# W_down's last row in two column pieces, and the output in column groups of 360 and 216

## The chip, the cores and the metric

The kernel runs on one core of a Trainium2 chip. The metric is the device time of one execution in microseconds (us). The kernel before takes 377.71 us, the median of three runs (377.70, 377.71 and 377.72).

## The reference

One decoding step of a transformer block for a batch of 4, in bfloat16: attention over the last 4096 positions of a cache (32 query heads on 16 key/value heads of 128), a residual, and then a gated feed-forward part whose last product is the one that the change touches. Cut to what matters:

```python
def _B_ref(x, W_gate, W_up, W_down):          # x: 4 x 1 x 576
    gate = jnp.einsum("bsd,df->bsf", x, W_gate)   # 576 x 4608
    up = jnp.einsum("bsd,df->bsf", x, W_up)       # 576 x 4608
    gate = gate * (gate > 0)
    h = gate * up
    return jnp.einsum("bsf,fd->bsd", h, W_down)   # 4608 x 576

x = A_x
h = x + _A_ref(_layernorm(x), A_k_cache, A_v_cache, A_wq, A_wo)
h2 = h + _B_ref(_layernorm(h), B_W_gate, B_W_up, B_W_down)
return h2
```

Of the caches and weights some 160 MB are read, each once.

## The kernel before, in words

The program writes the list of operations of every engine by hand. Each operation names what it depends on, and the function `emit` turns this into semaphore waits; an engine then works through its list in that order. All large transfers are issued from one queue, that of SyncE (SP), in the order in which `place` (line 216) is called. `place` also makes a transfer wait for the last reader of the part of the on-chip arena that it overwrites.

The work goes in this order. The query projection comes first. Then 16 tiles of K and 16 of V (4 MB each) pass through four slots of the arena: VectorE transposes a K tile (line 424), TensorE forms the scores, the softmax follows, and TensorE multiplies with V. Then come the output projection with Wo, the second layer norm (lines 627 to 647), the gate and up products (lines 651 to 677), and two transposes on VectorE (line 679), which lay the hidden vector out as 36 blocks of 128 (`hhT`).

The down projection is the last loop (lines 683 to 707). W_down's 4608 rows are laid out as 128 partitions of 36 rows each, so that a "row" r in the text is one row of 576 columns on each of 128 partitions, 147 KB. For each r from 0 to 35 there are two matmuls, n = 0 and n = 1, each with the same 128x32 stationary block of `hhT` and with its own share of the 576 columns as the moving operand. Group 0 (columns 0 to 271) writes to PSUM bank 0, partitions 0 to 31, and group 1 (columns 272 to 575) to bank 1, partitions 32 to 63; these positions put them in different 32-column strips of TensorE's array. Both accumulate over all 36 rows. Before row 0 come six matmuls that add the residual. In the last row the two weight loads are issued ahead of the matmuls (line 699), and the matmuls are made by `mm_same` (line 33), so that they are reported at line 34.

W_down arrives in five transfers, at rows 0, 15, 25, 32 and 35 (`WD_ROWS`, line 280); the matmul of group 0 at those rows waits for its piece. At the end VectorE copies group 0 to the output tile as bfloat16 (`OUT0`, line 708), ScalarE copies group 1 (`OUT1`, line 709), and SP sends the tile out when both are done (line 710).

Of the kernel before, what the change touches and what calls it, by code (L numbers as in the profile page):

```python
# [12 lines left out]
D = 576  # L13
# [19 lines left out]
def mm_same(e, out, lhsT, rhs, start, stop, tile, pos):  # L33
    return e.add_instruction(mybir.InstMatmult(  # L34
        name=e.bass.get_next_instruction_name(), engine=mybir.EngineType.PE, ins=[e.lower_ap(rhs), e.lower_ap(lhsT)],
        outs=[e.lower_ap(out)], start_tensor_calc=start, stop_tensor_calc=stop, tile_size=tile, tile_position=pos,
        ldweights=False, bass_skip_group_check=True))
# [83 lines left out]
def bass_sequential_preLN__sliding_block_cached__glu_gated_reglu__decode_kernel(  # L121
# [12 lines left out]
    with ExitStack() as es:  # L134
        cnt = [0]

        def sb(name, shape, dt):
            return es.enter_context(nc.sbuf_tensor("sb_" + name, shape, dt))
# [3 lines left out]
        dve = lambda name, fn, deps=(): P.op("vector", name, fn, deps)  # L142
        act = lambda name, fn, deps=(): P.op("scalar", name, fn, deps)
# [5 lines left out]
        arena = sb("arena", [128, AW], BF16)  # L149
# [41 lines left out]
        out_sb = sb("out_sb", [32, D], BF16)  # L191
# [14 lines left out]
        bank = [psb[:, i, :] for i in range(8)]  # L206
# [9 lines left out]
        def place(name, off, size, reader, make, key=None):  # L216
            deps = []
            for blk in range(off // 64, (off + size) // 64):
                r = owner.get(blk)
                if r is not None and r not in deps:  # L220
                    deps.append(r)
                owner[blk] = reader
            semk = key or "d_" + "_".join(str(v) for v in name)
            P.dma("sync", ("L",) + name, make, semk, deps)
            land[name] = off
# [37 lines left out]
        for g in range(NTILE - 4, NTILE):  # L263
# [6 lines left out]
            out=bass.AP(tensor=arena, offset=off, ap=[[2 * AW, 64], [1, F]]), in_=B_W_gate[512:576, :]))  # L270
        P.dma("sync", ("L", "gu", 1, 4), lambda e, off=off: e.dma_start(
            out=bass.AP(tensor=arena, offset=AW + off, ap=[[2 * AW, 64], [1, F]]), in_=B_W_up[512:576, :]), "d_gu_1_4")
        gu_off[(0, 4)] = gu_off[(1, 4)] = off
        off += F
        for g, m, n, src in ((0, 0, 4 * F, main_rows(B_W_gate)), (1, 0, 3 * F, main_rows(B_W_up)[:, 0:3 * F]),
# [1 line left out]
            gu_off[(g, m)] = off  # L277
            place(("gu", g, m), off, n, ("GU", g, m), lambda e, off=off, n=n, src=src: e.dma_start(out=arena[:, off:off + n], in_=src))
            off += n
        WD_ROWS = (0, 15, 25, 32, 35, 36)  # L280
        wd_off = off
        for r0, r1 in zip(WD_ROWS, WD_ROWS[1:]):
            place(("wd", r0), wd_off + r0 * D, (r1 - r0) * D, ("DOWN", 1),
                  lambda e, r0=r0, r1=r1: e.dma_start(
                      out=arena[:, wd_off + r0 * D:wd_off + r1 * D],
                      in_=B_W_down.rearrange("(p r) n -> p (r n)", p=128)[:, r0 * D:r1 * D]))


        pool("c_eps", lambda e: e.memset(eps_c[:, :], EPS))
# [15 lines left out]
                                                in_=c_qm[:, :, :].rearrange("p q (h j) -> p q h j", j=4),  # L305
# [4 lines left out]
                                                in_=to_v[:, :, :].rearrange("p n (k a) -> p n k a", a=4),  # L310
# [14 lines left out]
        for sg in range(2):  # L325
            pool(f"c_toq{sg + 1}", lambda e, sg=sg: e.affine_select(
                out=toq[:, :, :, :], in_=toq[:, :, :, :],
# [213 lines left out]
        def finish_o():  # L541
            for q in range(4):
                for qd in range(4):
# [17 lines left out]
                                              in_=bass.AP(tensor=e8, offset=0, ap=[[8, 128], [0, 4], [1, 8]])), ["c_e8", "c_selc0"])  # L561
# [47 lines left out]
        for a in range(8):  # L609
            for n in range(2):  # L610
                for j in range(4):
# [4 lines left out]
                    else:  # L616
# [6 lines left out]
                                             in_=bass.AP(tensor=psb, offset=512 + 224, ap=[[4096, 128], [1, 64], [0, 2]])), ["part1"])  # L623
# [27 lines left out]
        for g in range(2):  # L651
            for c in (4, 0, 1, 2, 3):
                part_ = c if c == 4 or (c == 3 and g) else 0
                for m in range(3):
                    for j in range(4):
                        first = m == 0 and j == 0 and (c in (0, 4) or part_ == 3)
                        deps = [("L", "gu", g, part_)] if first else []
                        if c == 4 and g == 0 and first:
                            deps += [("L", "gu", 1, 4), "n2", "n3", "part0", "partd", ("EXP", B - 1), ("MAX", B - 1)]
                        lo = gu_off[(g, part_)] + (c - part_) * F + 1152 * j + 384 * m  # L660
# [17 lines left out]
        for i in range(2):  # L678
            dve(("HHT", i), lambda e, i=i: e.transpose(
                out=hhT[:, 576 * i:576 * i + 576].rearrange("p (r q) -> p r q", q=32),  # L680
                in_=bass.AP(tensor=pp, offset=3712 + 18 * i, ap=[[PPW, 128], [1, 18], [36, 32]])), [("HH", m) for m in range(3)])

        ncol = ((0, 272), (272, 576))

        def down(n, lhsT, w, start, stop, held=False):
            lo, hi = ncol[n]
            out_ = bank[n][32 * n:32 * n + 32, 0:hi - lo]
            if held:
                return lambda e: mm_same(e, out_, lhsT, w[:, lo:hi], start, stop, (128, 32), (0, 32 * n))
            return lambda e: e.matmul(out_, lhsT=lhsT, rhs=w[:, lo:hi], start=start, stop=stop, skip_group_check=True)  # L690
# [5 lines left out]
        for r in range(36):  # L696
            if r == 35:
                for n in range(2):
                    pe(None, lambda e, n=n: e.ldweights(hhT[:, 32 * 35:32 * 36], tile_position=(0, 32 * n)))
            for n in range(2):  # L700
                deps = []
                if n == 0:
                    if r in WD_ROWS:
                        deps.append(("L", "wd", r))
                    if r % 18 == 0:
                        deps.append(("HHT", r // 18))
                pe(("DOWN", n), down(n, hhT[:, 32 * r:32 * r + 32], arena[:, wd_off + r * D:wd_off + r * D + D], False, r == 35, r == 35), deps)
        dve("OUT0", lambda e: e.tensor_copy(out=out_sb[:, 0:272], in_=bank[0][0:32, 0:272]), [("DOWN", 0)])
        act("OUT1", lambda e: e.copy(out=out_sb[:, 272:576], in_=bank[1][32:64, 0:304]), [("DOWN", 1)])  # L709
        P.dma("sync", "O", lambda e: e.dma_start(out=out.rearrange("b s d -> (b s) d"), in_=out_sb[0:B, :]), "d_out", ["OUT1", "OUT0"])  # L710
        P.op("sync", None, None, ["O"])
        P.emit(nc, es)
# [28 lines left out]
```

## Time and profile before

| | before |
|---|---|
| median of the runs | 377.71 us |
| span of the profiled execution | 377.0 us |
| mean granted TensorE clock | 0.796 of full speed |
| mean DMA rate over the span | 424 GB/s |
| TensorE matmul busy | 213.8 us (57%) |
| VectorE busy | 228.8 us (61%) |
| ScalarE busy | 53.7 us (14%) |
| last W_down piece issued, and its time to landing | 342.69 us, 32.0 us |
| output transfer issued | 375.64 us |

The profiled execution's own time is known only as its span, from its first to its last instruction; the runs are timed without a profile, and 0.7 us lie between the two. Times in the profile count from the start of the span. A busy share is an average over the whole execution and says little of its last stretch; there the chain of waits and the order of time are to be read. "PEclk" is the clock that TensorE was granted, as a share of full speed.

### The profile page before, as it was taken

What the parts mean: (1) busy time and instruction counts of PE and PEld (TensorE: products, weight loads), DVE (VectorE), ACT (ScalarE), POOL (GpSimd) and SP (SyncE); (2) the same over time, 40 slices, a digit from 0 to 9 for tenths busy, and PEclk for the clock granted to TensorE, in tenths of its full rate; (3) what the DMA queues carried; (4) which work ended last, traced back from release to release, by engine and by line L of the source; (5) the groups of instructions that cost most, each with busy time, mean ns of one, the idle gap of its engine ahead of it and who ended that gap; (6) DMA issues with size and microseconds to landing.
All of it is one profiled execution on the core that took longest, in us unless ns stands there. A gap on an engine that the chain in (4) does not pass through costs nothing.

```text
span 377.0 us, 2556 instructions
## 1 busy us (share of the span) xinstructions
PE 213.8 (57%) x1462; PEld 39.9 (11%) x694; DVE 228.8 (61%) x164; ACT 53.7 (14%) x84; POOL 10.5 (3%) x29
## 2 busy tenths in 40 slices
PE   0404443239919091749282844664655787886658
PEld 0000000001001010001010100110000101002316
DVE  4088878779292969584847778665749433333240
ACT  3093000211000114010101140101010411112010
POOL 8200000000000000000000000000000000000000
PEclk9966666659969788696877786989695968998686
DMA  8999999999999999999999999999999999999996
GB/s 334 445 445 428 405 445 442 396 442 445 398 435 445 442 433 403 442 445 435 407 436 445 435 414 431 441 438 431 417 442 438 426 417 442 418 433 437 427 414 256
DMA packets 6378, 159.74 MB, mean 424 GB/s; under 512 B 728, under 2 KB 864, under 8 KB 1248
## 3 DMA queue, kind: packets, MB, share of 16 engines
q1 hardware_dynamic: 6360, 159.59, 98.7%
q8 instruction: 8, 0.13, 0.1%
q14 instruction: 2, 0.02, 0.0%
q10 hardware_dynamic: 8, 0.00, 0.0%
HBM read 159.58 MB, written 0.00 MB: 423 GB/s over the span
## 4 chain that ended last, share of the span: by engine, by line
DMA 60%; PE 20%; DVE 18%; SPq 1%; issue 0%; ACT 0%
DMA sb_arena<-in_A_k_cache_dram 53%; DVE sb_arena L424 16%; PE psb L34 11%; DMA sb_arena<-in_B_W_down_dram 7%; PE psb L448 4%; PE psb L509 3%; PE psb L690 2%; DVE sb_o_tmp L522 1%; DVE sb_pp L487 1%; SPq L242 0%; PE psb L475 0%; SPq L255 0%; ACT sb_out_sb L709 0%; SPq L251 0%; DVE sb_f L534 0%
## 5 line engine op out<-in xcount | busy, mean ns | idle before, releaser
L424 DVE STREAM_TRANSPOSE sb_arena<-sb_arena 128x8192 f32<-128x8192 f32 (+1 forms) x19 | 139.9, 7366 | 67.3 <-DMA sb_arena<-in_A_k_cache_dram 67.3
L448 PE MATMUL psb<-sb_arena 128*32 128x512 bf16 x256 | 42.8, 633 | 119.6 <-DVE sb_arena L424 119.5
L34 PE MATMUL psb<-sb_arena,sb_pp 128*128 128x512 bf16 (+1 forms) x386 | 108.7, 392 | 0.0
L509 PE MATMUL psb<-sb_arena,sb_pp 128*128 128x512 bf16 x128 | 50.8, 397 | 8.9 <-DVE sb_o_tmp L522 8.9
L519 ACT COPY sb_o_tmp<-psb 32x512 f32<-32x512 f32 x32 | 18.5, 577 | 182.0 <-PE psb L34 181.7
L34 PE MATMUL psb<-sb_arena 128*32 128x512 bf16 x256 | 43.6, 642 | 0.0
L522 DVE TENSOR_TENSOR sb_o_tmp<-psb,sb_fm 32x512 f32<-32x512 f32 x32 | 21.7, 678 | 18.6 <-PE psb L34 18.1
L448 PEld LDWEIGHTS psb<-sb_arena 128*32 128x32 bf16 x256 | 9.5, 119 | 161.9 <-DVE sb_arena L424 132.7
L509 PEld LDWEIGHTS psb<-sb_arena,sb_pp 128*128 128x128 bf16 x128 | 12.8, 100 | 116.6 <-issue 116.6
L526 DVE TENSOR_REDUCE sb_o_sel<-sb_o_tmp 128x128 f32<-128x512 f32 x16 | 17.7, 1106 | 0.5
L467 ACT ACTIVATE sb_pp<-psb,sb_hx 128x1024 bf16<-128x1024 f32 x4 | 4.5, 1113 | 79.4 <-DVE sb_hx L464 79.4
L487 DVE TENSOR_TENSOR sb_pp<-psb,sb_m 128x1024 bf16<-128x1024 f32 x8 | 9.3, 1206 | 4.9 <-PE psb L475 4.9
L482 ACT ACTIVATE sb_pp<-psb,sb_m 128x512 bf16<-128x512 f32 x16 | 9.7, 690 | 14.9 <-PE psb L475 14.9
L525 DVE TENSOR_TENSOR sb_o_tmp<-sb_o_tmp,sb_fm 64x512 f32<-64x512 f32 x16 | 11.0, 689 | 0.5
L415 ACT COPY sb_arena<-sb_q_keep 32x256 bf16<-32x256 bf16 x8 | 9.7, 1451 | 0.1
L690 PE MATMUL psb<-sb_arena,sb_pp 128*32 128x272 bf16 (+1 forms) x70 | 7.6, 396 | 3.7 <-DMA sb_arena<-in_B_W_down_dram 3.7
L401 DVE CAST sb_pp<-psb 128x512 bf16<-128x512 f32 x1 | 2.4, 2427 | 10.5 <-PE psb L381 10.5
L470 DVE STREAM_TRANSPOSE sb_pp<-sb_pp 128x1024 bf16<-128x1024 bf16 x4 | 5.0, 1245 | 5.1 <-ACT sb_pp L467 5.1
L475 PE MATMUL psb<-sb_pp,sb_to_v 128*32 128x256 bf16 x64 | 4.3, 400 | 6.3 <-DVE sb_pp L470 6.3
L690 PEld LDWEIGHTS psb<-sb_arena,sb_pp 128*32 128x32 bf16 x70 | 6.0, 131 | 5.1 <-DMA sb_arena<-in_B_W_down_dram 3.9
L34 PE MATMUL psb<-sb_arena,sb_hnT 128*32 128x384 bf16 x80 | 6.5, 407 | 0.0
L381 PE MATMUL psb<-sb_arena,sb_xnT 128*32 128x512 bf16 x16 | 2.6, 628 | 6.3 <-DMA sb_arena<-in_A_wq_dram 6.3
(120 smaller groups left out, 81.5 us busy)
## 6 DMA issues: line engine op xcount, KB each, us to landing
sb_arena<-in_A_k_cache_dram SPq DMA_DIRECT2D x16, 4096.0 KB, 26.3
sb_arena<-in_A_v_cache_dram SPq DMA_DIRECT2D x16, 4096.0 KB, 28.5
sb_arena<-in_A_wo_dram SPq DMA_DIRECT2D x1, 4608.0 KB, 24.8
sb_arena<-in_B_W_gate_dram SPq DMA_DIRECT2D x1, 4608.0 KB, 27.7
sb_arena<-in_A_wq_dram SPq DMA_DIRECT2D x1, 4096.0 KB, 12.7
sb_arena<-in_B_W_up_dram SPq DMA_DIRECT2D x1, 3456.0 KB, 27.3
sb_arena<-in_B_W_down_dram SPq DMA_DIRECT2D x1, 2160.0 KB, 26.5
sb_arena<-in_B_W_down_dram SPq DMA_DIRECT2D x1, 1440.0 KB, 29.6
```

The costliest lines, as they stand in the source:

```text
L34: return e.add_instruction(mybir.InstMatmult(name=e.bass.get_next_instruction_name(), engine=mybir.EngineType.PE, ins=[e.lower_ap(rhs), e. ...
L415: act("QW", lambda e, i=i, q=q: e.copy(out=bass.AP(tensor=arena, offset=32 * i * AW + 2 * i + q, ap=[[AW, 32], [512, 16], [136, 4], [32, 4]]),
L424: dve(("TRA", g), lambda e: e.transpose(out=dst, in_=src), [("L", "K", g)] if lo == 0 else [])
L448: fn = lambda e, out_=out_, lhsT=lhsT, rhs=rhs, start=start, stop=stop: e.matmul(out_, lhsT=lhsT, rhs=rhs, start=start, stop=stop, skip_gr ...
L482: act(("EV", b, 0), lambda e, a=a: e.activation(out=bass.AP(tensor=pp, offset=2 * a, ap=[[PPW, 128], [8, 2], [32, 128], [1, 2]]), in_=bank ...
L487: dve(("EV", b, 1), lambda e, n=n: e.tensor_tensor(out=bass.AP(tensor=pp, offset=16 + 8 * n, ap=[[PPW, 128], [32, 128], [2, 4], [1, 2]]), ...
L509: fn = lambda e, lhsT=lhsT, rhs=rhs, k=k, j=j: e.matmul(bank[2 + j], lhsT=lhsT, rhs=rhs, start=(k == 0), stop=(k == 7), skip_group_check=True)
L519: act(("OSC", g), lambda e, j=j: e.copy(out=o_tmp[32 * j:32 * j + 32, 0:512], in_=bank[2 + j][32 * j:32 * j + 32, :]), [("PV", g), ("OSEL" ...
L522: dve(("OSD", g), lambda e, j=j: e.tensor_tensor(out=ot(32 * j, 32), in0=bank[2 + j][32 * j:32 * j + 32, :].rearrange("p (t d) -> p t d", ...
L525: dve(("OS", g), lambda e: e.tensor_tensor(out=ot(64, 64), in0=ot(64, 64), in1=fmb(64, 64), op=ALU.mult), [("OSC", g)])
L526: dve(("OSEL", g), lambda e: e.tensor_reduce(out=o_sel[:, qd, b, :], in_=o_tmp[:, 0:512].rearrange("p (t d) -> p d t", d=DH), axis=AX.X, o ...
L690: return lambda e: e.matmul(out_, lhsT=lhsT, rhs=w[:, lo:hi], start=start, stop=stop, skip_group_check=True)
```

## The change

The output's two column groups become 0 to 359 and 360 to 575 (360 and 216 columns) in place of 272 and 304. This holds for all 36 rows, for the residual's matmuls, and for the two copies at the end. W_down's row pieces start at rows 0, 15, 28 and 33, and row 35 comes as two transfers of its own, one for each column group (360 and 216 columns). In row 35 each group's matmul waits for its own piece.

```diff
-        WD_ROWS = (0, 15, 25, 32, 35, 36)
+        WD_ROWS = (0, 15, 28, 33, 35)
+        SPLIT = 360
         wd_off = off
         for r0, r1 in zip(WD_ROWS, WD_ROWS[1:]):
             place(("wd", r0), wd_off + r0 * D, (r1 - r0) * D, ("DOWN", 1),
...
+        for n, (lo, hi) in enumerate(((0, SPLIT), (SPLIT, D))):
+            place(("wd", 35, n), wd_off + 35 * D + lo, hi - lo, ("DOWN", 1),
+                  lambda e, lo=lo, hi=hi: e.dma_start(
+                      out=arena[:, wd_off + 35 * D + lo:wd_off + 35 * D + hi],
+                      in_=B_W_down.rearrange("(p r) n -> p (r n)", p=128)[:, 35 * D + lo:35 * D + hi]))
...
-        ncol = ((0, 272), (272, 576))
+        ncol = ((0, SPLIT), (SPLIT, D))
...
                 if n == 0:
-                    if r in WD_ROWS:
+                    if r in WD_ROWS and r < 35:
                         deps.append(("L", "wd", r))
                     if r % 18 == 0:
                         deps.append(("HHT", r // 18))
+                if r == 35:
+                    deps.append(("L", "wd", 35, n))
...
-        dve("OUT0", lambda e: e.tensor_copy(out=out_sb[:, 0:272], in_=bank[0][0:32, 0:272]), [("DOWN", 0)])
-        act("OUT1", lambda e: e.copy(out=out_sb[:, 272:576], in_=bank[1][32:64, 0:304]), [("DOWN", 1)])
+        dve("OUT0", lambda e: e.tensor_copy(out=out_sb[:, 0:SPLIT], in_=bank[0][0:32, 0:SPLIT]), [("DOWN", 0)])
+        act("OUT1", lambda e: e.copy(out=out_sb[:, SPLIT:D], in_=bank[1][32:64, 0:D - SPLIT]), [("DOWN", 1)])
```

## The prediction

> **What bounds the kernel now.** I read the chain of waits first, then the order of time over the last 15 us, then the transfers by time to landing, then the shapes of the last loop's matmuls, and last the granted clock by 3.41 us stretches, because the chain ends in TensorE and not in a transfer.
>
> The chain that ended last, its last pieces:
>
> ```profile
> 340.90 26.55 DMA sb_arena<-in_B_W_down_dram
> 367.45 0.04 issue
> 367.49 7.54 PE psb L690 x66
> 375.04 0.15 PE psb L34
> 375.21 0.40 ACT sb_out_sb L709
> ```
>
> Up to 367.45 the transfers set the time; the first W_down piece lands and the down projection runs 7.7 us without a break in the chain. From then on it is TensorE, then the ScalarE copy of the second column group, then the output transfer. The same stretch in order of time:
>
> ```profile
> 367.49 7.55 PE L690 MATMUL psb<-sb_arena,sb_pp 128*32 128x272 bf16 x70 [3.72 <-DMA sb_arena<-in_B_W_down_dram]
> 374.64 0.21 PEld L699 LDWEIGHTS <-sb_pp 128*32 128x32 bf16 x2
> 374.76 0.42 PE L34 MATMUL psb<-sb_arena,sb_pp 128*32 128x272 bf16 x2
> 375.10 0.43 DVE L708 CAST sb_out_sb<-psb 32x272 bf16<-32x272 f32 x1 [8.36 <-PE psb L34]
> 375.21 0.40 ACT L709 CAST sb_out_sb<-psb 32x304 bf16<-32x304 f32 x1 [13.62 <-PE psb L34]
> 375.64 0.33 SPq L710 DMA_DIRECT2D out_dram<-sb_out_sb  x1
> ```
>
> The transfers, with KB and us from issue to landing:
>
> ```profile
> sb_arena<-in_B_W_down_dram SPq DMA_DIRECT2D x1, 1440.0 KB, 29.6
> sb_arena<-in_B_W_down_dram SPq DMA_DIRECT2D x1, 1008.0 KB, 31.5
> ...
> sb_arena<-in_B_W_down_dram SPq DMA_DIRECT2D x1, 432.0 KB, 32.1
> sb_arena<-in_B_W_down_dram SPq DMA_DIRECT2D x1, 144.0 KB, 32.0
> ```
>
> They are issued at 341.27, 341.74, 342.22 and 342.69, so they land at about 370.9, 373.3, 374.3 and 374.7. So the last row (144 KB) is there just when TensorE reaches it at 374.76: transfers and TensorE finish almost together.
>
> The matmuls of the loop by shape, between 367.4 and 373.3, and the granted clock (us, PE busy, PEclk, DMA share, GB/s):
>
> ```profile
> L690 PE MATMUL psb<-sb_arena,sb_pp 128*32 128x304 bf16 x24 | 6.1, 454 | 0.0
> L690 PE MATMUL psb<-sb_arena,sb_pp 128*32 128x272 bf16 x25 | 5.9, 432 | 3.7 <-DMA sb_arena<-in_B_W_down_dram 3.7
> ```
>
> ```profile
> 363.12:366.54 3.42, 0.65 (x6) 1.00 0.96 402
> 366.54:369.95 3.41, 2.46 (x21) 0.50 1.01 428
> 369.95:373.36 3.41, 3.41 (x32) 0.50 0.89 366
> 373.36:375.20 1.84, 1.82 (x25) 1.00 0.20 74
> ```
>
> Two things are to be seen. The two column groups stand in different 32-column strips of the array and run beside each other: their starts are 0.2265 us apart for 272 columns and 0.2535 for 304 at clock 0.50, and 0.116 and 0.129 at 1.00. A row thus costs what its **wider** group costs, not the sum of both; the 304-column stream never pauses, while the 272-column stream has slack and waits for transfers. And 5.87 us of this loop run at half clock, after the idle stretch before it; full clock comes only at 373.36. As a test, (5.87 + 0.03 for the shorter first step) / 0.2535 = 23.3 rows at half clock, and the 11.7 left until row 35 starts take 1.51 us: 374.87, where the trace has 374.88.
>
> **The change, part by part.**
>
> *The wider group grows from 304 to 360 columns, in all 36 rows.* From the spacings above a column costs (0.2535 - 0.2265)/32 = 0.00084 us at half clock and 0.0004 at full. 360 columns: 0.3005 us and 0.1525 us a row. Until 373.36: 5.90 / 0.3005 = 19.6 rows. Left until row 35: 15.4 x 0.1525 = 2.34 us, so it starts at 375.70. The other group (216 columns, 0.180 us) runs beside it and no longer counts. The last matmul that paces moves from 374.88 to 375.70.
>
> *The copy out.* VectorE (L708) now takes the late group. It started 0.34 us after its last matmul; 88 columns more add 0.037 at full clock: 376.08. Its duration is 0.428 for 32x272; the 32x512 operation of L522 (0.68) gives 1.04 ns a column, so 0.52; bounds 0.43 (no growth) and 0.59 (the slope to 128x288 at L620, 0.458). I take 0.52, the slope over the longer reach: done at 376.60. ScalarE's 216 columns take about 0.33 (slope to 32x512 at L519, 0.577) and end near 376.34, beside it. The output transfer followed ScalarE's copy by 0.025 us and the VectorE signal took 0.028 to reach SP; between 0.025 and 0.1 I take 0.06: issue at 376.66 instead of 375.64.
>
> *The sum.* +1.02 us on the output transfer, which itself is unchanged (1.3 us to the end). The profiled span is 377.0 (376.96 by the chain's clock) against a median of 377.71, so some 0.75 lie outside; 377.71 + 1.02 = **378.7 us**.
>
> *The pieces of W_down.* Rows 15-27 now come as one piece instead of 15-24. At 0.342 us a row (10 rows between 367.45 and 370.87) and 0.346 for the next, they land at about 371.90; the 360-column stream asks for row 15 at 367.77 + 14 x 0.3005 = 371.97. The wait moves from slack to within 0.07 us of the pacing stream; nothing to +0.1 us, I take 0. The pieces after it land at about 373.65, 374.3 and 374.8 and are asked for at 374.6, 375.4 and 375.70: the waits at rows 25 and 32 go, those at 28, 33 and 35 are met early, so splitting the last row has no waiting left to remove. Its 16 smaller packets for each engine in place of 8 cost between nothing and as much again as the 8 (0.05 us each, 0.4); the 0.9 us that TensorE is late covers all of it.
>
> *What is free.* One more issue on SP's queue (0.47 us between issues, near 343.2) has only the output transfer behind it, 33 us later; without that cover it would cost 0.47. The residual matmuls of 362.86-363.8 get wider by some 0.1 us in front of a 3.7 us idle stretch. The second wait at row 35 stands in front of the last 216-column matmul alone; its transfer is long there.
>
> **Rivals.**
>
> 1. *The clock is released earlier in the timed runs* (not slower by what can be measured). In the profile the release at 373.36 is the end of a full busy stretch of 3.41 us; if the stretches began elsewhere, it could be 370.9. TensorE would then run ahead and be held by the larger piece at 371.94; 20 rows x 0.1525 bring row 35 to 374.99, 0.71 earlier than in my sum: +0.3, **378.05**. It decides once the release is before about 372.8. The kernel before would hardly show it, since its last row waits for 374.7 in any case, so three runs within 0.02 us do not exclude it. Against it: those runs fit one fixed phase as well, and then the profile holds. The Trainium skill, "TensorE: Matmul & The Clock Gate", Part 1, says that this window of 3413 ns is free-running and does not restart with the kernel; by that rule the release wanders over a window and my +1.02 would be one draw between about +0.3 and +1.3. One profile can't show that; the stretches of 3.41 us agree.
>
> 2. *The clock is not released at 373.36*, because one of the two streams now idles 28% of the time. Release a stretch later (376.78) would put row 35 at 377.4: +1.7 more, **380.4**. Against it: a single stream without pause was enough earlier:
>
> ```profile
> 305.10:308.51 3.41, 3.41 (x10) 0.50 1.01 432
> 308.51:311.92 3.41, 3.41 (x17) 1.00 1.05 452
> ```
>
> 3. *The transfers bound the end and the split pays* (faster): the 360-column piece lands a little before the rest and its copy starts while 216 columns are still on their way. That needs TensorE ahead of the transfers all along, which the half clock forbids; even then only the last row's 0.13 us and part of a 0.4 us copy are to be had: **377.5**. Faster by over 0.2% (0.76 us, about what a measurement of this kernel can tell from no change) would need a third of the 2.25 us left after the last landing.
>
> **How the numbers follow.** My forecast with the release near 373.4: 0.72, its own range 378.45 to 379.1 (the wait at row 15 up to +0.1, the copy -0.1 to +0.1, SP -0.03 to +0.04, the release up to 0.4 us later or earlier at half that price). Rival 1: 0.20. Rival 2: 0.04. Rival 3: 0.04. The range must reach to rival 1 and so runs from 377.95 to 379.1. Slower by over 0.2% (above 378.47): nearly all of the forecast, and rival 2, 0.75. Within 0.2%: rival 1, most of rival 3 and a sliver of the forecast, 0.22. Faster: 0.03.
>
> **What would show it.** In the changed profile: L690's 360-column matmuls start 0.30 us apart at clock 0.50 and 0.15 at 1.00, without a pause but at row 15; row 35 starts near 375.7, a microsecond after the last W_down piece has landed; VectorE's copy takes 0.52 us, and is the last thing before the output transfer, with ScalarE's done before it. The forecast is wrong if the clock rises before 372.8, if a pause of over 0.1 us stands at row 15, or if the chain ends in a W_down transfer.

## The result, and the profile after

The changed kernel takes 378.18 us (median of 21 runs, 378.00 to 379.92) beside 377.70 for the kernel before (21 runs, 377.55 to 377.97). The ratio is 1.0017 with a 95% interval of 1.0011 to 1.0023: slower, by 0.5 us at the median, and by less than the 0.2% that was called a measurable change. As telling as the median is the scatter. In these runs the kernel before stays within 0.4 us; the changed one has 12 runs from 378.0 to 378.2 and then a tail up to 379.1, with one run at 379.92.

The changed kernel's profiled execution has a span of 376.85 us, shorter than the 376.96 of before, although the kernel is slower: its W_down transfers landed 0.4 us earlier, and its clock rose earlier. Each run on record after the prediction has its own time and its own span beside each other, and the time is 1.20 to 1.33 us the longer in all of them. The profiled execution of the changed kernel (376.85) took 378.10; by the same difference the 376.96 of the profile before belong to an execution of some 378.2 us, longer than every one of the 21 runs of that kernel. So the profile before is not of a typical execution: the 0.7 us between its span and the median of the runs are two executions compared, not a part of one that the profile leaves out. The chain that ended last, from its last transfer on:

```profile
337.54 33.93 DMA sb_arena<-in_B_W_down_dram
371.47 0.04 issue
371.51 3.07 PE psb L696 x26
...
374.93 0.51 DVE sb_out_sb L716
```

The chain no longer leaves the transfers at 367.5 but at 371.47, when the second piece (rows 15 to 27) lands. The same place in order of time:

```profile
367.04 3.89 PE L696 MATMUL psb<-sb_arena,sb_pp 128*32 128x360 bf16 x30 [3.60 <-DMA sb_arena<-in_B_W_down_dram]
371.51 3.07 PE L696 MATMUL psb<-sb_arena,sb_pp 128*32 128x360 bf16 x39 [0.58 <-DMA sb_arena<-in_B_W_down_dram]
374.57 0.32 PE L34 MATMUL psb<-sb_arena,sb_pp 128*32 128x360 bf16 x1
374.93 0.52 DVE L716 CAST sb_out_sb<-psb 32x360 bf16<-32x360 f32 x1 [8.63 <-PE psb L34]
374.95 0.33 ACT L717 CAST sb_out_sb<-psb 32x216 bf16<-32x216 f32 x1 [16.40 <-PE psb L34]
375.54 0.33 SPq L718 DMA_DIRECT2D out_dram<-sb_out_sb  x1
```

And the granted clock by 3.41 us stretches (us, TensorE busy, PEclk, DMA share, GB/s):

```profile
366.56:369.98 3.42, 2.94 (x23) 0.50 0.99 421
369.98:373.39 3.41, 2.83 (x37) 1.00 0.84 332
```

The clock rises (it is released, in the prediction's word) at 369.98, not at 373.36. TensorE is through rows 0 to 14 by 370.9, waits for row 15, and then needs 20 rows x 0.1525 us = 3.05 us to row 35. VectorE's copy of 360 columns is the last work before the output transfer, and ScalarE's is done before it.

### The profile page after: what moved, and what is told of

Same layout as the page of the kernel before. It is cut to its first block, busy times and chain, and to the rows that moved or that the text cites. A ratio compares the mean times of both kernels' runs of the same rounds, so it can differ in the third digit from the quotient of the medians.

```text
span 376.8 us, 2542 instructions
## 1 busy us (share of the span) xinstructions
PE 208.3 (55%) x1447; PEld 38.9 (10%) x694; DVE 227.7 (60%) x164; ACT 53.6 (14%) x84; POOL 10.7 (3%) x29
## 4 chain that ended last, share of the span: by engine, by line
DMA 62%; DVE 18%; PE 18%; SPq 1%; issue 1%
DMA sb_arena<-in_A_k_cache_dram 53%; DVE sb_arena L430 16%; PE psb L34 11%; DMA sb_arena<-in_B_W_down_dram 9%; PE psb L454 4%; PE psb L515 2%; DVE sb_o_tmp L528 1%; PE psb L696 1%; DVE sb_pp L493 1%; SPq L242 0%; PE psb L481 0%; DVE sb_out_sb L716 0%; SPq L255 0%; SPq L251 0%; SPq L285 0%
## 5 line engine op out<-in xcount | busy, mean ns | idle before, releaser
L454 PE MATMUL psb<-sb_arena 128*32 128x512 bf16 x256 | 43.9, 637 | 119.6 <-DVE sb_arena L430 119.5
L34 PE MATMUL psb<-sb_arena,sb_pp 128*128 128x512 bf16 x384 | 105.1, 381 | 2.4 <-issue 2.3
L515 PE MATMUL psb<-sb_arena,sb_pp 128*128 128x512 bf16 x115 | 44.0, 383 | 8.9 <-DVE sb_o_tmp L528 8.9
L34 PE MATMUL psb<-sb_arena 128*32 128x512 bf16 x256 | 44.8, 645 | 0.0
L696 PE MATMUL psb<-sb_arena,sb_pp 128*32 128x216 bf16 (+1 forms) x70 | 7.1, 336 | 4.2 <-DMA sb_arena<-in_B_W_down_dram 4.2
L681 DVE TENSOR_TENSOR sb_pp<-psb,sb_pp 128x384 bf16<-128x384 f32 x3 | 1.5, 549 | 9.5 <-PE psb L672 9.5
L672 PE MATMUL psb<-sb_arena,sb_hnT 128*32 128x384 bf16 x40 | 4.2, 405 | 4.5 <-DMA sb_arena<-in_B_W_up_dram 2.5
## 6 DMA issues: line engine op xcount, KB each, us to landing
sb_arena<-in_A_wq_dram SPq DMA_DIRECT2D x1, 4096.0 KB, 12.8
```

The lines of the kernel that those rows point to most:

```text
L34: return e.add_instruction(mybir.InstMatmult(name=e.bass.get_next_instruction_name(), engine=mybir.EngineType.PE, ins=[e.lower_ap(rhs), e. ...
L454: fn = lambda e, out_=out_, lhsT=lhsT, rhs=rhs, start=start, stop=stop: e.matmul(out_, lhsT=lhsT, rhs=rhs, start=start, stop=stop, skip_gr ...
L515: fn = lambda e, lhsT=lhsT, rhs=rhs, k=k, j=j: e.matmul(bank[2 + j], lhsT=lhsT, rhs=rhs, start=(k == 0), stop=(k == 7), skip_group_check=True)
```

## The experiments

The theory after this result: the wider group paces the loop, and what that costs depends on where the 3.41 us window of the clock falls in an execution. The rival: the new W_down transfers (the larger piece at row 15, the split last row) make the loss, whatever the widths. The first four kernels ran on one chip, where the kernel before took 378.06 us (35 runs, 377.66 to 378.53); the other four on another, where it took 377.76 (27 runs, 377.59 to 378.62, all but two of them below 378.0). Each ratio is against the runs on the same chip. On both the kernel before itself scatters over 0.9 to 1.0 us, so a spread of that size is no sign of the change by itself.

**The groups alone.**

```diff
+        SPLIT = 360
...
-        ncol = ((0, 272), (272, 576))
+        ncol = ((0, SPLIT), (SPLIT, D))
```

with the copies to match, and W_down as before.

> Groups of 360 and 216 alone; W_down in the five old transfers (rows 0, 15, 25, 32, 35). Theory 'width' (the 360-column stream paces at 0.3005 us a row at half clock and 0.1525 at full, and the release of the clock falls anywhere in a 3.41 us window): 0.15 to 0.35 us over the kernel before at the median, lowest runs about +0.15, and a tail of runs up to +1.3. Rival 'pieces' (the larger piece at row 15 and the split last row make the loss): 377.7, no change, no tail.

Measured: 378.52 us (11 runs, 378.10 to 379.18), ratio 1.0012 (1.0004 to 1.0021), +0.46 at the median, which by the interval may be +0.15 to +0.79. The median is above the 0.15 to 0.35 that was expected, and the tail (378.52 to 379.18) is little longer than the scatter of the kernel before on this chip. The widths alone give a loss of the changed kernel's size.

**The transfers alone.**

```diff
-        WD_ROWS = (0, 15, 25, 32, 35, 36)
+        WD_ROWS = (0, 15, 28, 33, 35)
```

with row 35 in two pieces of 272 and 304 columns, and the groups as before.

> The new W_down transfers alone (rows 0, 15, 28, 33 and the last row in two column pieces), groups of 272 and 304 as before. Theory 'width': median within 0.15 us of the kernel before, some runs up to +0.6, since 304 columns make up the later row 15 at full clock (20 rows x 0.129 = 2.6 us after 371.9 gives 374.5, before the last landing). Rival 'pieces': the whole loss of the change, +0.4 to +0.5.

Measured: 378.10 us (11 runs, 377.73 to 378.66), ratio 1.0002 (0.9993 to 1.0010), which is at most +0.38 us. The rival falls: the pieces cost nothing that can be measured at these widths, although TensorE waits for row 15 here too. The chain of this kernel:

```profile
371.83 0.04 issue
371.88 2.91 PE psb L696 x39
374.78 0.27 PE psb L34 x2
375.05 0.02 issue
375.07 0.40 ACT sb_out_sb L717
```

With 304 columns the 20 rows after the wait need 2.6 us of their own (20 x 0.129). They take 2.9 with short waits at rows 28, 33 and 35, and row 35 of the wide group starts at 374.74, 0.04 us after the last piece has landed (374.70). Whether the pieces add something at 360 columns is not shown: the groups alone and the whole change did not run on the same chip.

**The clock held up before row 0.** In the changed kernel, after the residual's matmuls:

```diff
+        for _ in range(14):
+            pe(None, lambda e: e.matmul(bank[7], lhsT=ident_b[:, :], rhs=arena[:, WO_OFF:WO_OFF + 512], start=True, stop=True, skip_group_check=True))
         for r in range(36):
```

> The changed kernel with 14 additional 128x512 matmuls, whose result nobody reads, between the residual's matmuls and row 0, where TensorE waits 3.7 us for W_down, so that the clock is not taken down before row 0. Theory 'free clock window': the loop runs at full clock in every execution, the runs lie within 0.3 us of each other around 378.0 (row 15 waits for its piece at 371.9, 20 rows x 0.1525 bring row 35 to 375.0). Rival 'the runs scatter for another reason' (transfers): the same scatter as the changed kernel, 378.0 to 379.1.

Measured: 378.67 us (12 runs, 377.96 to 380.46), ratio 1.0025 (1.0013 to 1.0038). A miss: not narrower but wider, with four runs between 379.8 and 380.5. The profiled execution did what was expected. In order of time, and then by stretches:

```profile
363.85 3.20 PE L703 MATMUL psb<-sb_arena,sb_ident_b 128*128 128x512 bf16 x14
367.53 2.46 PE L696 MATMUL psb<-sb_arena,sb_pp 128*32 128x360 bf16 x30 [0.48 <-DMA sb_arena<-in_B_W_down_dram]
371.99 3.07 PE L696 MATMUL psb<-sb_arena,sb_pp 128*32 128x360 bf16 x39 [2.00 <-DMA sb_arena<-in_B_W_down_dram]
```

```profile
365.10:368.51 3.41, 2.93 (x27) 1.00 1.01 430
368.51:371.92 3.41, 1.48 (x17) 1.00 0.95 400
371.92:375.34 3.42, 3.35 (x42) 1.00 0.46 170
```

Full clock throughout, and row 35 at 375.05. But a loop at full clock runs into the wait at row 15 sooner and stands for 2.0 us there. In this execution almost the whole pause lies in one stretch (368.51 to 371.92, TensorE busy for 1.48 of 3.41 us), and the clock stayed up. In the profile of the kernel before, the clock went down after a stretch with about as much work in it (342.66 to 346.07, 1.55 us busy), so a pause of this kind may take it down in another execution. Then the last 21 rows would run for up to 3.41 us at half clock and lose 1.7 us. That is an argument, and it fits the 380s; the last experiment tests whether they hang on the pause.

**The same matmuls in the kernel before.**

> The kernel before with the same 14 additional matmuls. Theory 'free clock window': 377.65, no change beyond 0.1 us, because its end is set by the last landing, with the runs a little closer together. Rival 'the half clock holds the kernel before as well': 0.3 us or more faster.

Measured: 378.15 us (11 runs, 378.04 to 378.44), ratio 1.0005 (0.9996 to 1.0014). No gain, so the half clock does not hold the kernel before. And no run lies near 380, so the 14 matmuls alone do not make such runs.

**Groups of 432 and 144**, with the old transfers: the same edit as the first, one size further.

> Groups of 432 and 144, W_down in the five old transfers. Theory 'width': the wide stream takes 0.360 us a row at half clock and 0.1825 at full; lowest runs +0.7 over the kernel before, median +1.0, a tail up to +2.4; so more than twice the loss of 360 and 216 alone (+0.46 measured). If only the copy at the end counts (0.60 us of VectorE for 432 columns), +0.2 and no tail.

Measured: 379.53 us (5 runs, 378.65 to 380.13), ratio 1.0047 (1.0034 to 1.0059). The lowest run is +0.89 and the median +1.77, more than expected (+0.7 and +1.0); the tail reaches as far as expected. The copy alone (0.59 us) can't give this. In the profile the clock rose at 371.58: (4.57 + 0.03) / 0.360 = 12.8 rows at half clock and 22.2 x 0.1825 = 4.05 us bring row 35 to 375.63:

```profile
375.64 0.35 PE L34 MATMUL psb<-sb_arena,sb_pp 128*32 128x432 bf16 x1
376.03 0.59 DVE L709 CAST sb_out_sb<-psb 32x432 bf16<-32x432 f32 x1 [9.78 <-PE psb L34]
```

The expectation of the median took an early release as the usual case. One profile and five runs don't show how the releases of this kernel were spread. An estimate: by the two paces a release 1 us later costs 1 - 0.1825 / 0.360 = 0.49 us, so the 1.48 us from the lowest run to the highest would be releases 3.0 us apart, most of a stretch.

**The changed kernel once more.**

> The changed kernel once more, beside the others on one chip. Theory 'width with a free clock window': +0.3 to +0.6 at the median, runs spread over about 1 us upwards; its profile shows a release of the clock at another place than the profiles so far, and either a pause at row 15 (release before about 371.9) or an unbroken 360-column stream (later).

Measured: 378.32 us (11 runs, 377.99 to 379.02), ratio 1.0018 (1.0009 to 1.0027), +0.56 at the median: the first result again. Its profiled execution took 378.86 and has the late release that the first one lacked:

```profile
366.05:369.47 3.42, 2.34 (x19) 0.50 0.97 414
369.47:372.88 3.41, 3.41 (x26) 0.50 0.90 364
372.88:375.60 2.72, 2.72 (x33) 1.00 0.20 68
```

```profile
367.13 8.02 PE L696 MATMUL psb<-sb_arena,sb_pp 128*32 128x360 bf16 x68 [3.61 <-DMA sb_arena<-in_B_W_down_dram]
...
375.29 0.32 PE L34 MATMUL psb<-sb_arena,sb_pp 128*32 128x360 bf16 x1
375.64 0.52 DVE L716 CAST sb_out_sb<-psb 32x360 bf16<-32x360 f32 x1 [9.26 <-PE psb L34]
```

There is no pause at row 15, and row 35 starts at 375.29. So the same program has shown its release at 369.98 and at 372.88, and its end by both cases of the prediction.

**Groups of 288 and 288**, with the old transfers.

> Groups of 288 and 288, W_down in the five old transfers. Theory 'width': 0.240 us a row at half clock; within 0.1 us of the kernel before at the median, since the last landing sets the end of both, and a highest run that is no higher than that of the kernel before. If narrower groups shorten the end by themselves: 0.2 us or more faster.

Measured: 377.80 us (11 runs, 377.63 to 378.18), ratio 1.0000 (0.9991 to 1.0009). A narrower wide group brings nothing, as expected, because the last landing then sets the end.

**The clock held up before row 0 and before row 15.** As the third, and nine more of these matmuls in front of row 15.

> The changed kernel with the 14 additional matmuls before row 0 and nine more of the same before row 15, where the kernel with the 14 alone stood 2.3 us at full clock. Theory: the runs near 380 of that kernel were executions in which this pause took the clock down again; with the pause filled they go, all runs lie within 0.5 us of each other, and the median is 0.2 to 0.4 over the kernel before. Rival 'additional matmuls themselves cost, or the transfers scatter': runs near 380 remain.

Measured: 378.16 us (11 runs: ten from 378.01 to 378.19, one at 378.71), ratio 1.0010 (1.0001 to 1.0018). The 380s are gone, and so, but for one run, is the tail that the changed kernel showed on this chip; that one run breaks the expectation that all lie within 0.5 us. (The 2.3 us of the expectation count from the start of row 14 to that of row 15; the wait itself was 2.0.) But the 380s were seen on the other chip, and the kernel with the 14 matmuls alone did not run on this one, so it is not shown that filling the pause is all that removed them. The additional matmuls fill the wait at row 15:

```profile
369.50 2.12 PE L709 MATMUL psb<-sb_arena,sb_ident_b 128*128 128x512 bf16 x9
371.57 3.07 PE L696 MATMUL psb<-sb_arena,sb_pp 128*32 128x360 bf16 x39
```

Row 15 starts 0.04 us after its piece has landed (371.53), so these nine cost nothing. What remains, +0.40 us (+0.04 to +0.68 by the interval), is what the change costs when the loop runs at full clock: most of the loss at the median. The half clock makes most of the tail.

The profiles side by side, in us. Landings differ by 0.6 us between executions (374.66 to 374.81 in the four on the first experiments' chip, 374.17 to 374.42 in the four on the other), so the last column, from the last W_down landing to the issue of the output transfer, is the one to compare:

| kernel | clock rises | row 0 starts | last W_down landing | wide group's row 35 starts | landing to output issue |
|---|---|---|---|---|---|
| before | 373.36 | 367.49 | 374.72 | 374.88 | 0.93 |
| after, first profile | 369.98 | 367.04 | 374.32 | 374.57 | 1.21 |
| after, second profile | 372.88 | 367.13 | 374.42 | 375.29 | 1.84 |
| groups 360/216 alone | 370.79 | 367.43 | 374.66 | 374.81 | 1.12 |
| transfers alone | 371.41 | 367.40 | 374.70 | 374.74 | 0.80 |
| after, 14 matmuls more | stays up | 367.53 | 374.81 | 375.05 | 1.21 |
| after, 14 and 9 more | stays up | 367.11 | 374.40 | 374.63 | 1.20 |
| before, 14 more | stays up | 367.60 | 374.81 | 374.89 | 0.88 |
| groups 432/144 | 371.58 | 367.01 | 374.23 | 375.64 | 2.49 |
| groups 288/288 | 371.38 | 366.94 | 374.17 | 374.23 | 0.91 |

With the groups at 360 the end comes 0.2 to 0.9 us later after the last landing, by the place of the release; with 272/304 or 288/288 it is 0.8 to 0.93 wherever the release falls. Of the 0.40 us that remain at full clock this column has 0.27 (1.20 against 0.93); the profiles do not show the rest.

A check of the theory, as an estimate from these numbers: if the release comes R us after row 0, the paces of 0.3005 and 0.1525 us a row alone put row 35 of the changed kernel at 5.32 + 0.49 R after row 0; the wait at row 15 puts it at 7.53 (367.04 to 374.57). The two meet at R = 4.5. The profiles have R from 2.9 to 5.9; if it falls evenly between them, half of the executions should lie together at the lowest times and the others up to 0.7 us above. Of the 21 runs 12 lie within 0.2 us of the lowest, and eight more up to 1.07 above it: the share fits, and the tail is somewhat longer than the release alone gives.

## Why the prediction was right, and where it failed

- *The wider group paces the loop* held. With the second profile's own start and release, the prediction's working gives (5.75 + 0.03) / 0.3005 = 19.2 rows and 15.8 x 0.1525 = 2.41 us, row 35 at 375.29; measured 375.29. In this profile there is no pause at row 15, as forecast.
- *The copy out* held: 0.52 us on VectorE, 0.33 on ScalarE beside it. The step from VectorE's end to the output transfer was 0.09 us, inside its bounds (0.025 to 0.1) and 0.03 over the value taken.
- *The pieces* held: the 13-row piece landed 4.47 us after the first (4.45 worked out), and the transfers alone gave 1.0002. The wait at row 15 was priced at nothing for a late release; for an early one rival 1 had it, with row 35 3.05 us after the piece, as the trace shows (371.51 to 374.57).
- *The chances failed.* The forecast gave 0.72 to a release near 373.4 in the timed runs, and with it 378.7 us and "slower by over 0.2%". The median, 378.18, lies near rival 1 (378.05; 378.02 by its own terms), which had 0.20. In the first profile two of the prediction's own signs of being wrong are there: the clock rose before 372.8, and a pause of 0.58 us stands at row 15, whose wait the sum took as 0. In the second profile neither is. The step that failed is the reading of the three runs within 0.02 us as support for a fixed phase. The prediction itself had said that the kernel before would hardly show a moving release; so they were no evidence, and the profile's release was one draw, from the late end. The rule of the Trainium skill ("TensorE: Matmul & The Clock Gate", Part 1), that this window runs freely and does not restart with the kernel, was set beside it and given too little weight; two profiles of the same program, with releases at 369.98 and 372.88, agree with it. In the seven profiles whose loop began at half clock, the first boundary of a stretch after row 0 came anywhere from 0.59 to 3.36 us behind it. In the sum the term is the 5.90 us at half clock: the changed kernel showed 2.94 and 5.75.
- *The time outside the span* was mis-sized: 0.75 us in the sum, 1.20 to 1.33 in all later runs. The +1.02 is a difference within one execution and does not change by that. But it was worked out for an execution of some 378.2 us, which with it comes to 379.2, and it was added to the median of executions 0.5 us shorter.
- *The range* (377.95 to 379.1) holds the median and 20 of the 21 runs, because it had been drawn out to rival 1. Rival 2 stands in no profile: each had full clock by 373.4. (Its reason, a stream that idles 28% of the time, is misworked: 0.180 of 0.3005 us leave 40%.) The one run at 379.92 lies 1.7 us above the typical ones, as a clock down for one more stretch would have it; it has no profile. Rival 3 did not come about: no run of the changed kernel was below 377.99.

What stays open: a clock that goes down in the pause at row 15 is inferred from the 380s and from their absence, on another chip, once the pause was filled; no profile caught it, and the one profile with a pause of 2.0 us kept its clock. The run of the changed kernel at 379.92 may have the same cause; that was not shown. Nor was it shown what the pieces add at 360 columns, or why the kernel before scatters more on the two other sets of runs than in the first.

## What to carry to other kernels

Matmuls that ran beside each other in two column strips cost here what the wider strip costs; split an output evenly among such strips unless something later needs it otherwise, and ask what the strip costs at half clock. After an idle stretch of TensorE this loop began at half clock for anything from 2.9 to 5.9 us: for a loop like it, work out its end for an early and for a late release, and let the result be a range. Equal times of a kernel that is bound by transfers say nothing of a clock that it does not feel.

## What the runs showed of the hardware

- The clock can rise after a stretch in which TensorE was not busy throughout, and the share of busy time alone does not decide it. In the down projection the clock stayed down after 68% (366.05 to 369.47, the changed kernel's second profile) and 72% (366.54 to 369.95, the kernel before), and it rose after 86% (366.56 to 369.98, the changed kernel's first profile). The first profile's row 0 started 0.45 us earlier than that of the kernel before, by an earlier landing, in a stretch that began at almost the same time, and its release came 3.4 us earlier. But earlier in that same trace the clock rose after 46% (284.64 to 288.06, 1.58 us busy) and went down after 76% (346.08 to 349.50, 2.60 us busy). What else counts is not shown.
- Holding the clock up can make a loop stand longer at its next wait: at full clock row 14 started 2.1 us after row 0 (367.53 to 369.67) instead of 3.6 (367.04 to 370.61), and the wait at row 15 was 2.0 us instead of 0.58. Four of that kernel's twelve runs (379.84 to 380.46) stood 0.9 us and more above the other eight (377.96 to 378.90); that the longer wait did it was not caught in a profile.
- The strips are not in step: group 0's matmul of row 24 (372.92) began before group 1's of row 22 (373.04), which stands in front of it in the program. But the narrow group does not run far ahead: in the changed kernel's first profile the 216-column group gains three rows (its row 8 starts at 368.52, the wide group's row 5 at 368.51) and from there its starts are 0.300 us apart, like the wide group's. With 432 and 144 columns it is three rows as well (367.71 and 367.70).
